# Reordering the opening of a fused attention and mixture kernel, and moving a few preparation steps of later head pairs

## The chip, the core and the metric

The kernel runs on one core of a Trainium2 chip. The metric is device microseconds (us) of one execution, the median of a few runs. The engines are named as the profile names them: PE is the matrix engine, PEld its weight loads, DVE the vector engine, ACT the scalar (activation) engine, POOL the general engine, and SP the queue from which all of this kernel's DMAs are issued. Each engine works through its own list of instructions in order; an instruction that waits holds up everything behind it in its list.

## What is computed

Three stages follow each other, all in float32:

```python
q_assign = argmax(normalize(q) @ normalize(centroids).T)      # 16 clusters, per head
k_assign = argmax(normalize(k) @ normalize(centroids).T)
mask     = q_assign[:, None] == k_assign[None, :]
scores   = where(mask, q @ k.T / sqrt(64), -1e9)               # 2 x 8 heads, 768 x 768
x        = softmax(scores) @ v                                 # tokens x 512
h        = x @ w_in;  x = (max(h, 0) + alpha * min(h, 0)) @ w_out
xn       = x / rms(x) * rms_g
out      = (silu(xn @ w_gate) * (xn @ w_val)) @ w_out2
```

## The kernel before, in words

Attention works on 8 pairs of heads (`pr` 0 to 7), the two large matrix stages follow it. The order of all instructions is written out by hand: `Attention.setup` issues the opening, then `Attention.plan` puts every further step at a slot and an order within the slot, and the slots from -12 on are issued one after the other. Pair `pr` owns slots 12·pr to 12·pr+11; a slot holds the score tiles of one block of 128 keys for the two heads of a pair. The tables `THIRD`, `FOURTH` and `FIFTH` (pairs 2, 3 and 4) give the places of preparation steps relative to the pair's own first slot: an entry (-24, 4) of pair 3 stands in slot 12, after whatever has an order below 4 there.

A pair is prepared so. `load` fetches q and k, transposed (`raw`, through L456) and natural (`nat`, L454). `prep_sq` squares them on ACT (L469), and the sums of squares give the norms (`root` in the opening, L399 to L409; `rnorm` for later pairs). `prep_hi` rounds `raw` to the matrix engine's format into `stage` (L606 on ACT, for pair 0 L608 on DVE), `prep_lo` writes the residual of the rounding beside it (L614). `sims_mm` (L516) multiplies with the centroids, `sims_copy` (L521) and `sims_turn` (L527) bring the result into token order, `prep_scale` (L543) divides by the norms, and `prep_arg` (L552 to L565) makes one-hot codes `oh` of the best cluster. DMAs copy rounded values and residuals into the operands `op1` and `op2` (`prep_dma_a` L618, `prep_dma_b` L626 to L630). The codes have to get into rows 64 to 79 of `op1`; for pairs 0 and 1 that is on PE and ACT: for pair 0 `oht_direct(h)` turns the codes of head `h` by 12 small matmuls (L589) and copies them with ACT (L598 the k side, L600 the q side).

Only then can a pair start: `max_tile` (L662) multiplies rows 0 to 79 of `op1`, and DVE takes the row maximum (L666 for the first six tiles of head pair 0, L664 later), which becomes two more operand rows (`max_split` L671 to L672, `max_rows` L690, `rows_copy` L699). `st_tile` (L712, L713) makes scores, ACT takes exp (L714), `pv_tiles` (L728, L739) multiplies with v and sums.

In the opening the PE list is: `warm(6)` (L393, matmuls on zeros), a turn of the centroid norms (L348), `sims_mm(0)`, `ss_rows(0)` (L494, sums of squares over partitions), `ss_turn` (L503), `sims_turn(0)`, `spread` of the centroids (L325), `warm(3)`, `sims_mm(1)`, `ss_rows(1)`, `ss_turn` for pair 1, `warm(4)`, `oht_direct(0)`, `oht_direct(1)`, first `max_tile`. The PSUM buffers named `ps_st` are three, given out in turn: the buffer of `ss_turn` for pair 1 is the same one into which `oht_direct(1)` puts its last three of 12 matmuls. `root` for pair 1 reads that buffer on ACT (L399 and, since it keeps a copy, L403).

Of the kernel before, what the change touches and what calls it, by code (L numbers as in the profile page):

```python
# [12 lines left out]
AF = mybir.ActivationFunctionType  # L13
ALU = mybir.AluOpType
# [4 lines left out]
BIG = float(2.0 ** 60)  # L19
# [15 lines left out]
FIFTH = {  # L35
    **PAIR,
    "lo": ((-26, 2.3), (-25, 1.05)),
    "load": ((-41, 6.1), (-41, 6.2), (-39, 6.1), (-38, 6.1)),
    "sq": ((-35, 4), (-34, 4)),
    "ss": ((-34, 5), (-33, 5)),  # L40
}
FOURTH = {
    **PAIR,
    "load": ((-38, 6.1), (-38, 6.2), (-30, 6.1), (-30, 6.2)),
    "sq": ((-32, 4), (-32, 4.1)),
    "ss": ((-30, 2.2), (-30, 2.3)),
    "norm": tuple((-27 + n // 6, 5 + (n % 6) / 10) for n in range(17)),
    "hi": ((-27, 4), (-26, 4)),
# [9 lines left out]
    "sq": ((-24, 4), (-23, 4)),  # L58
    "ss": ((-24, 5), (-23, 5)),
    "norm": tuple((-21, 5.1 + n / 100) for n in range(14)) + tuple((-18, 2.41 + n / 100) for n in range(3)),  # L60
    "hi": ((-22, 4), (-21, 4)),
    "lo": ((-18, 2.46), (-14, 6)),
    "sims": ((-20, 1.65), (-18, 1.7)),
    "scale": ((-18, 2.44),),
    "arg": ((-18, 2.45), (-16, 5), (-16, 5.1), (-15, 5), (-14, 5)),
# [160 lines left out]
class Attention:  # L226
# [52 lines left out]
    def setup(self):  # L279

        nc, C, H, D = self.nc, self.C, self.H, self.D
        v, act, g = nc.vector, nc.scalar, nc.gpsimd
        n, rows = H * C, 2 * C
        cn = self.pre([n, 2, D], "cn")
        css = self.pre([n, 1], "css")
        self.sq0 = self.pre([128, D], "sq0")
        src = self.centroids.rearrange("h c d -> (h c) d")
# [29 lines left out]
        i = self.idf.rearrange("p (e g r) -> p g e r", e=2, r=32)  # L317
        hi, lo = (i[..., r:r + 1].to_broadcast([128, 2, 2, 64]) for r in range(2))
# [3 lines left out]
        def spread(cb, w, copy):  # L322

            ps = self.bk.pr()
            nc.tensor.transpose(ps[:, :w], cn[:w].rearrange("p a d -> p (a d)"), self.idf[:w, :w])  # L325
            src = ps[:, :w].rearrange("p (j e c) -> p j e c", e=2, c=C)
            for e in range(2):
                copy(out=cb[64 * e:64 * e + 64, :, C * e:C * e + C], in_=src[64 * e:64 * e + 64, :, e, :])
# [4 lines left out]
        steps, r = self.root(css, [n, 1], "c")  # L333
        self.warm(3, self.bk.pv)
        spread(self.cb0.unsqueeze(1), rows, v.tensor_copy)
        for step in steps:
            step()
        for i in range(2):
            self.prep_sq(0, i)
        self.prep_hi(0, 0)  # L340
        self.prep_lo(0, 0)
        for i in range(2):
            v.tensor_scalar(out=cn[:, i, :], in0=cn[:, i, :], scalar1=r, scalar2=None, op0=ALU.mult)
        self.prep_hi(0, 1)
        self.warm(6, self.bk.pv)
        rc = self.bk.st()
        for i in range(0, 128, rows):
            nc.tensor.matmul(rc[i:i + rows, 0:1], lhsT=self.idf[:rows, :rows], rhs=r[:rows], start=True, stop=True)  # L348
        act.copy(out=self.rc0, in_=rc[:, 0:1])
        ps = self.bk.pr()  # L350
        self.sims_mm(0, ps)
        self.prep_sq(1, 0)
        simc = self.sims_copy(0, ps, self.rc0)
        ssc = self.ss_rows(0, v.tensor_copy)
        for h in range(2):
            self.prep_dma_a(h)
        for h in range(2):
            self.prep_dma_b(h, 1)
        self.load_v(0)
        steps, rn = self.root(self.ss_turn(ssc), [128, self.T // 2, 4, 2], "n0")  # L360
        self.sims_turn(0, self.bk.st(), simc)
        spread(self.cb, n, act.copy)
        self.prep_sq(1, 1)
        for step in steps:
            step()
        self.norm[0] = None, rn
# [4 lines left out]
        ps = self.bk.st()  # L371
        self.sims_mm(1, ps)
        ssc = self.ss_rows(1, act.copy)
        self.simc[1] = self.sims_copy(1, ps, 1.0)
        self.norm[1] = self.root(self.ss_turn(ssc), [128, self.T // 2, 4, 2], "n1", True)
        act.add_instruction(mybir.InstLoadActFuncSet(name=nc.get_next_instruction_name(), act_func_set_id=EXP_AND_LN,
                                                     ins=[], outs=[]))
        act.activation(out=spare, in_=self.eps[:, 0:1], func=AF.Exp)
        self.warm(4, self.bk.pv)
        self.prep_lo(0, 1)  # L380
        for h in range(2):
            self.oht_direct(h)
        for i in range(2):
            self.prep_hi(1, i)
        v.tensor_tensor_reduce(out=pat, in0=pat, in1=self.idf, scale=1.0, scalar=0.0, op0=ALU.mult, op1=ALU.add,
# [191 lines left out]
    def oht_direct(self, h):  # L577

        nc, X = self.nc, self.T // 2
        if h:  # L580
            hi = [self.bk.pr(), self.bk.st()]
            ps = [[self.bk.st(), self.bk.st()], hi]
        else:
            ps = [b().rearrange("p a b -> p (a b)") for b in (self.bk.mx, self.bk.pv)]
            ps = [[b, b[:, self.HS:]] for b in ps]
        for i in (1, 0):
            for g in range(2):
                for x in range(X):
                    nc.tensor.matmul(ps[i][g][0:16, x * 128:(x + 1) * 128], lhsT=self.oh[0][:, x, h, :, i, g],  # L589
                                     rhs=self.idr, start=True, stop=True)  # L590
        o1 = self.op1[h][64:80]
        for i in (1, 0):
            cuts = ((0, 128), (128, self.S)) if not i else ((0, self.S),)
            parts = [(ps[i][g][:16, :self.HS], o1[:, i, sl]) for g, sl in self.halves()] if h else \
                [(ps[i][0][:16, a:b], o1[:, i, a:b]) for a, b in cuts]
            for src, dst in parts:
                if i:
                    nc.scalar.copy(out=dst, in_=src)  # L598
                else:
                    nc.scalar.activation(out=dst, in_=src, func=AF.Identity, scale=-BIG)  # L600

# [198 lines left out]
    def plan(self):  # L800
# [3 lines left out]
        def at(s, o, fn, *a):  # L804
            ev.setdefault(s, []).append((o, len(ev.get(s, [])), fn, a))
# [4 lines left out]
        for pr in range(self.NP):  # L810
            b = SLOTS * pr
            tab = (FIRST, SECOND, THIRD, FOURTH, FIFTH, PAIR)[min(pr, 5)]
            for key, fn in (("load", self.load), ("sq", self.prep_sq), ("ss", self.prep_ss), ("hi", self.prep_hi),
                            ("lo", self.prep_lo), ("sims", self.prep_sims), ("scale", self.prep_scale),
                            ("norm", self.prep_norm), ("arg", self.prep_arg), ("oht", self.prep_oht),
                            ("load_v", self.load_v)):
                for n, to in enumerate(tab.get(key, ())):
                    if to:
                        at(b + to[0], to[1], fn, pr, n)
            h = 2 * pr  # L820
            if pr == 0:
                at(-12, -1, self.prep_dma_b, 0, 2)
                at(-12, 1, self.prep_dma_b, 1, 2)
            elif pr == 1:
                at(-5, 12, self.prep_dma_a, h)
                at(-4, 12, self.prep_dma_a, h + 1)
                at(5, 2.8, self.prep_dma_oh, h)
                at(5, 2.8, self.prep_dma_oh, h + 1)
                at(6, 2.8, self.prep_dma_b, h)
                at(6, 2.8, self.prep_dma_b, h + 1)  # L830
            else:
                for e in range(2):
                    at(b - 12, 2.5, self.prep_dma_a, h + e)
                    at(b - 12, 2.5, self.prep_dma_oh, h + e)
                    at(b - 11 + e, 2.5, self.prep_dma_b, h + e)
# [539 lines left out]
```

## Time and profile before

| | us |
|---|---|
| median of 3 runs | 819.69 (819.63 to 819.71) |
| the profiled execution | 819.63 |
| its span, first to last instruction | 817.9 |
| PE busy | 809.6 (99%) |
| DVE busy | 623.7 (76%) |
| ACT busy | 335.6 (41%) |
| POOL busy | 362.1 (44%) |

Busy times of PE contain modelled ends of pipelined matmuls, so that neighbours overlap; the distance from start to start is what one costs the list. A timeline row is start, duration, engine, line, operation, destination and source, shapes, the count of merged instructions, and in brackets the idle time before it with what ended it.

### The profile page before, as it was taken

Reading aid. Unit: us, or ns where it says so; the run is one execution under the profiler, and the core shown is the slowest. Engines: PE = TensorE matmul, PEld = TensorE weight load, DVE = VectorE, ACT = ScalarE, POOL = GpSimd, SP = SyncE. Lnnn points to the kernel's source line nnn. Section 1 sums busy time; section 2 is a strip of 40 time slices with the busy share of each in tenths; the row PEclk is TensorE's granted clock in tenths of the full one; section 3 lists DMA queues with packets and bytes.
Section 4 is the critical chain, followed back from the end, with each engine's and each line's share of the span. In section 5 each row is a group of like instructions: output and inputs, shape, how many; then the busy total and the mean of one; then the engine's idle time right before and its main releaser. Section 6 shows DMA issues by size and latency. Waiting matters only on the chain.

```text
span 817.9 us, 11705 instructions
## 1 busy us (share of the span) xinstructions
PE 809.6 (99%) x4350; PEld 625.0 (76%) x4350; DVE 623.7 (76%) x1036; ACT 335.6 (41%) x652; POOL 362.1 (44%) x335
## 2 busy tenths in 40 slices
PE   8999999999999999999999999999999999999998
PEld 5565666666666888888888888888888888888887
DVE  6989999999998489999999977877555555555523
ACT  7655776666564333433434444432212221222110
POOL 3421221221213267786766772416465546554511
PEclk9999999999999999999999999999999999999999
DMA  8786655754532022232212220102121212121012
GB/s 206 201 229 181 132 154 161 171 111 115 133 114 79 1 77 78 78 103 65 88 59 75 77 78 1 51 1 78 52 77 54 76 52 77 57 73 51 1 52 103
DMA packets 23624, 74.03 MB, mean 91 GB/s; under 512 B 3600, under 2 KB 4752, under 8 KB 23568
## 3 DMA queue, kind: packets, MB, share of 16 engines
q1 hardware_dynamic: 23568, 73.29, 31.3%
q8 instruction: 34, 0.56, 0.3%
q14 instruction: 22, 0.18, 0.1%
HBM read 49.88 MB, written 3.15 MB: 65 GB/s over the span
## 4 chain that ended last, share of the span: by engine, by line
PE 96%; DVE 2%; DMA 1%; ACT 1%; issue 0%; SPq 0%; DVEq 0%; ACTq 0%
PE ps_st L1010 35%; PE ps_mx L1010 14%; PE ps_pv L1010 14%; PE ps_pv L728 8%; PE ps_pr L1010 5%; PE ps_st L712 4%; PE ps_st L713 4%; PE ps_sm L739 3%; PE ps_ma L662 3%; PE ps_mb L662 2%; DMA nat<-in_kn_dram 1%; DVE mx L666 1%; PE ps_pv L393 1%; PE ps_pr L516 1%; PE ps_pr L690 0%; PE ps_pr L782 0%
## 5 line engine op out<-in xcount | busy, mean ns | idle before, releaser
L1077 POOL TENSOR_TENSOR gl<-v,gh 128x512 fp32r<-128x512 f32 x68 | 96.0, 1412 | 143.8 <-ACT gh L1076 142.4
L1076 ACT CAST gh<-v 128x512 fp32r<-128x512 f32 x68 | 42.3, 622 | 151.9 <-DVE v L1073 83.3
L1073 DVE TENSOR_TENSOR v<-ps_st,t 128x512 f32<-128x512 f32 x36 | 24.9, 691 | 100.3 <-PE ps_st L1010 100.2
L714 ACT ACTIVATE p<-ps_st 128x384 f32<-128x384 f32 x192 | 85.3, 491 | 28.1 <-PE ps_st L713 26.6
L992 DVE SCALAR_TENSOR_TENSOR dec_a<-raw,dec_a 128x512 uint32<-128x512 uint32 x66 | 81.6, 1236 | 2.2
L728 PE MATMUL ps_pv<-p,vnat 128*64 128x384 f32 x384 | 72.6, 499 | 0.0
L1069 DVE SCALAR_TENSOR_TENSOR v<-v,alpha,t 128x512 f32<-128x512 f32 x45 | 53.0, 1177 | 21.9 <-ACT v L1068 21.8
L712 PE MATMUL ps_st<-op 128*128 128x384 f32 x192 | 67.8, 353 | 0.3 <-ACT oht L575 0.3
L1010 PE MATMUL ps_st<-x1h,stage 128*128 128x512 f32 x272 | 67.2, 389 | 0.0
L713 PE MATMUL ps_st<-op 82*128 82x384 f32 x192 | 65.0, 339 | 0.0
L1010 PEld LDWEIGHTS ps_st<-x1h,stage 128*128 128x128 f32 x272 | 51.1, 188 | 10.6
L1123 DVE TENSOR_TENSOR x<-ps_mx,x 128x1024 f32<-128x1024 f32 x36 | 43.9, 1220 | 18.7 <-PE ps_mx L1010 18.7
L664 DVE TENSOR_REDUCE mx<-ps_ma 128x1 f32<-128x384 f32 x90 | 49.7, 552 | 10.1 <-PE ps_ma L662 9.2
L798 POOL TENSOR_TENSOR x1l<-X,x1h 128x384 fp32r<-128x384 f32 x15 | 15.9, 1062 | 91.7 <-ACT x1h L795 91.7
L1010 PE MATMUL ps_st<-x1h,wvh 128*128 128x512 f32 x144 | 56.2, 390 | 0.0
L1010 PE MATMUL ps_st<-x1h,wvl 128*128 128x512 f32 x144 | 56.0, 389 | 0.0
L1010 PE MATMUL ps_st<-x1h,wih 128*128 128x512 f32 x132 | 51.6, 391 | 0.0
L1010 PE MATMUL ps_st<-x1h,wil 128*128 128x512 f32 x132 | 51.4, 389 | 0.0
L664 DVE TENSOR_REDUCE mx<-ps_mb 128x1 f32<-128x384 f32 x90 | 49.4, 549 | 0.1
L1123 DVE TENSOR_TENSOR x<-ps_pv,x 128x1024 f32<-128x1024 f32 x35 | 42.5, 1214 | 6.8 <-PE ps_pv L1010 6.8
L990 DVE TENSOR_SCALAR dec_a<-raw 128x512 uint32<-128x512 uint32 x66 | 47.6, 722 | 0.0
L995 DVE SCALAR_TENSOR_TENSOR dec_e<-raw,dec_e 128x512 f32<-128x512 uint32 x66 | 45.7, 692 | 2.3
(304 smaller groups left out, 1998.3 us busy)
## 6 DMA issues: line engine op xcount, KB each, us to landing
raw<-in_moe_w_out_dram SPq DMA_DIRECT2D x28, 512.0 KB, 3.5
op<-stage SPq DMA_DIRECT2D x32, 384.0 KB, 5.9
raw<-in_moe_w_in_dram SPq DMA_DIRECT2D x15, 512.0 KB, 3.6
raw<-in_moe_w_val_dram SPq DMA_DIRECT2D x12, 512.0 KB, 3.4
raw<-in_moe_w_gate_dram SPq DMA_DIRECT2D x12, 512.0 KB, 3.4
op<-stage SPq DMA_DIRECT2D x16, 288.0 KB, 5.9
raw<-in_qt_dram SPq DMA_DIRECT2D x8, 384.0 KB, 4.8
raw<-in_kt_dram SPq DMA_DIRECT2D x8, 384.0 KB, 5.1
```

The costliest lines, as they stand in the source:

```text
L664: nc.vector.tensor_reduce(out=mx[:, g, k:k + 1], in_=to, op=ALU.max, axis=AX.X)
L712: nc.tensor.matmul(ps, lhsT=o1[:, 1, ks], rhs=o1[:, 0, qs], start=True, stop=False)
L713: nc.tensor.matmul(ps, lhsT=o2[:, 1, ks], rhs=o2[:, 0, qs], start=False, stop=True)
L714: nc.scalar.activation(out=self.P[s][:, e], in_=ps, func=AF.Exp, scale=self.scale)
L728: nc.tensor.matmul(ps[64 * e:64 * e + 64], lhsT=self.vnat[ph // 2][:, e, t0 + y], rhs=P[y][:, e], start=t0 + y == 0, stop=t0 + y == T - 1)
L990: lambda: v.tensor_scalar(out=a, in0=top, scalar1=3, scalar2=0x3FFFFFFF, op0=ALU.logical_shift_left, op1=ALU.bitwise_and),
L992: lambda: v.scalar_tensor_tensor(out=a, in0=top, scalar=0xC0000000, in1=a, op0=ALU.bitwise_and, op1=ALU.bitwise_or),
L995: lambda: v.scalar_tensor_tensor(out=ef, in0=bot, scalar=2.0 ** -52, in1=ef, op0=ALU.mult, op1=ALU.mult),
L1010: self.nc.tensor.matmul(ps, lhsT=a, rhs=b, start=first and i == 0, stop=last and i == len(terms) - 1)
L1069: nc.vector.scalar_tensor_tensor(out=v, in0=v, scalar=self.nalpha[:, a], in1=t, op0=ALU.mult, op1=ALU.add)
L1077: nc.gpsimd.tensor_tensor(out=lo, in0=v, in1=f(hi), op=ALU.subtract)
L1123: nc.vector.tensor_tensor(out=dst, in0=ps, in1=dst, op=ALU.add)
```

## The change

- Opening: the squares of pair 0's k are cut in two halves, one for ACT and one for DVE; `prep_hi(0, 1)` follows at once; both residuals of pair 0 come directly after it; the centroids are scaled by ACT instead of DVE; `ss_rows(0)` goes ahead of the turn of the centroid norms and of `sims_mm(0)` and is copied by ACT; `sims_copy(0)` comes after the first two steps of `root`, both squares of pair 1 after `spread`; the second half of `prep_dma_b(0)` moves from slot -12 to ahead of `load_v`.
- End of the opening: `oht_direct(0)` now comes before `root` for pair 1, and the load of the exp function set after `oht_direct(1)`; the copies of `oht_direct` are cut into halves and shared between ACT and DVE.
- Pair 2: rounding of k from slot 3 to slot 2, residual of q from slot 6 to slot 12. Pair 3: squares of q from slot 4 to slot 3. Pair 4: the two loads of `raw` from slots 9 and 10 to slot 13.

```diff
 FIFTH = {
-    "load": ((-41, 6.1), (-41, 6.2), (-39, 6.1), (-38, 6.1)),
+    "load": ((-41, 6.1), (-41, 6.2), (-35, 2.7), (-35, 2.8)),
 FOURTH = {
-    "sq": ((-32, 4), (-32, 4.1)),
+    "sq": ((-33, 4), (-32, 4)),
 THIRD = {
-    "hi": ((-22, 4), (-21, 4)),
-    "lo": ((-18, 2.46), (-14, 6)),
+    "hi": ((-22, 4), (-22, 4.1)),
+    "lo": ((-12, 2.02), (-14, 6)),
...
-        for i in range(2):
-            self.prep_sq(0, i)
-        self.prep_hi(0, 0)
-        self.prep_lo(0, 0)
+        self.prep_sq(0, 0)
+        self.prep_hi(0, 0)
+        sq, raw = self.nat[0][:, 1].rearrange("p t h d -> p (t h d)"), self.raw[0][:, 1]
+        (_, s0), (_, s1) = self.halves()
+        act.activation(out=sq[:, s0], in_=raw[:, s0], func=AF.Square)
+        v.tensor_tensor(out=sq[:, s1], in0=raw[:, s1], in1=raw[:, s1], op=ALU.mult)
+        self.prep_hi(0, 1)
         for i in range(2):
-            v.tensor_scalar(out=cn[:, i, :], in0=cn[:, i, :], scalar1=r, scalar2=None, op0=ALU.mult)
-        self.prep_hi(0, 1)
+            act.activation(out=cn[:, i, :], in_=cn[:, i, :], func=AF.Identity, scale=r)
+        for i in range(2):
+            self.prep_lo(0, i)
         self.warm(6, self.bk.pv)
+        ssc = self.ss_rows(0, act.copy)
         rc = self.bk.st()
...
         self.sims_mm(0, ps)
-        self.prep_sq(1, 0)
-        simc = self.sims_copy(0, ps, self.rc0)
-        ssc = self.ss_rows(0, v.tensor_copy)
...
+        self.prep_dma_b(0, 2)
         self.load_v(0)
         steps, rn = self.root(self.ss_turn(ssc), [128, self.T // 2, 4, 2], "n0")
-        self.sims_turn(0, self.bk.st(), simc)
+        self.sims_turn(0, self.bk.st(), self.sims_copy(0, ps, self.rc0))
         spread(self.cb, n, act.copy)
-        self.prep_sq(1, 1)
+        for i in range(2):
+            self.prep_sq(1, i)
...
         self.simc[1] = self.sims_copy(1, ps, 1.0)
-        self.norm[1] = self.root(self.ss_turn(ssc), [128, self.T // 2, 4, 2], "n1", True)
+        ss = self.ss_turn(ssc)
+        self.warm(4, self.bk.pv)
+        self.oht_direct(0)
+        self.norm[1] = self.root(ss, [128, self.T // 2, 4, 2], "n1", True)
+        self.oht_direct(1)
         act.add_instruction(mybir.InstLoadActFuncSet(name=nc.get_next_instruction_name(), act_func_set_id=EXP_AND_LN,
                                                      ins=[], outs=[]))
         act.activation(out=spare, in_=self.eps[:, 0:1], func=AF.Exp)
-        self.warm(4, self.bk.pv)
-        self.prep_lo(0, 1)
-        for h in range(2):
-            self.oht_direct(h)
...
+        cuts = (0, 128), (128, self.S)
         for i in (1, 0):
-            cuts = ((0, 128), (128, self.S)) if not i else ((0, self.S),)
-            parts = [(ps[i][g][:16, :self.HS], o1[:, i, sl]) for g, sl in self.halves()] if h else \
+            parts = [(ps[i][g][:16, :self.HS], o1[:, i, sl]) for g, sl in self.halves()] if h or i else \
                 [(ps[i][0][:16, a:b], o1[:, i, a:b]) for a, b in cuts]
-            for src, dst in parts:
+            for n, (src, dst) in enumerate(parts):
+                aside = n == (1 if i else 0) and (i or not h)
                 if i:
-                    nc.scalar.copy(out=dst, in_=src)
+                    (nc.vector.tensor_copy if aside else nc.scalar.copy)(out=dst, in_=src)
+                elif aside:
+                    nc.vector.tensor_scalar(out=dst, in0=src, scalar1=-BIG, scalar2=None, op0=ALU.mult)
                 else:
                     nc.scalar.activation(out=dst, in_=src, func=AF.Identity, scale=-BIG)
...
             if pr == 0:
-                at(-12, -1, self.prep_dma_b, 0, 2)
                 at(-12, 1, self.prep_dma_b, 1, 2)
```

## Rows read from the trace of the kernel before

**Rows 1.** The page: part 1 (busy us, shares), part 4 (chain by engine), part 6 (loads).

```profile
PE 809.6 (99%) x4350; PEld 625.0 (76%) x4350; DVE 623.7 (76%) x1036; ACT 335.6 (41%) x652; POOL 362.1 (44%) x335
PE 96%; DVE 2%; DMA 1%; ACT 1%; issue 0%; SPq 0%; DVEq 0%; ACTq 0%
...
raw<-in_qt_dram SPq DMA_DIRECT2D x8, 384.0 KB, 4.8
```

**Rows 2.** Busy time by stretch: stretch, length; PE, PEld, DVE, ACT, POOL; clock, DMA share, GB/s.

```profile
0.00:10.00 10.00, 7.87 (x44) 4.67 (x44) 5.53 (x18) 5.94 (x13) 7.21 (x45) 1.00 0.61 187
17.00:23.00 6.00, 5.35 (x27) 3.78 (x27) 5.86 (x11) 4.16 (x9) 0.00 (x0) 1.00 1.03 194
23.00:30.00 7.00, 6.70 (x44) 3.90 (x45) 6.41 (x16) 4.62 (x8) 3.73 (x8) 1.00 1.04 312
```

**Rows 3.** The chain that ended last, in order of time: start, us, what.

```profile
13.71 1.28 ACT L376
15.24 0.79 ACT op L598
16.24 0.64 PE ps_pv L662 x2
16.90 2.70 DVE mx L666 x3
```

**Rows 4.** Timeline of PE in the opening.

```profile
3.26 2.93 PE L393 MATMUL ps_pv<-zero 128*128 128x512 f32 x6
7.05 0.82 PE L494 MATMUL ps_st<-nat,hs 128*32 128x384 f32 x8
8.56 0.55 PE L503 MATMUL ps_st<-idf,ssc 128*128 128x128 f32 x3 [0.69 <-DVE ssc L496]
8.94 0.49 PE L527 MATMUL ps_st<-idf,simc 128*128 128x128 f32 x3
9.27 0.27 PE L325 MATMUL ps_pr<-idf,cn 128*128 128x128 f32 x1
12.42 0.55 PE L503 MATMUL ps_st<-idf,ssc 128*128 128x128 f32 x3 [0.58 <-ACT ssc L496]
12.72 1.17 PE L393 MATMUL ps_pv<-zero 128*128 128x512 f32 x4
14.21 0.52 PE L589 MATMUL ps_pv<-idr,oh 128*16 128x128 f32 x6 [0.31 <-DVE oh L565]
```

**Rows 5.** Timeline of ACT in the opening.

```profile
4.80 1.81 ACT L469 ACTIVATE nat<-raw 128x768 f32<-128x768 f32 x2 [1.12 <-DMA raw<-in_qt_dram]
9.14 0.28 ACT L399 ACTIVATE n_y<-ps_st,eps 128x24 f32<-128x24 f32 x1 [0.87 <-PE ps_st L503]
10.11 0.84 ACT L469 ACTIVATE nat<-raw 128x768 f32<-128x768 f32 x1
11.89 0.48 ACT L496 COPY ssc<-ps_st 128x384 f32<-128x384 f32 x1 [0.94 <-PE ps_st L494]
13.54 0.16 ACT L403 COPY n_s<-ps_st 128x24 f32<-128x24 f32 x1
18.27 1.57 ACT L606 CAST stage<-raw 128x768 fp32r<-128x768 f32 x2
```

**Rows 6.** Timeline of DVE in the opening.

```profile
10.78 0.56 DVE L543 TENSOR_TENSOR sims<-ps_st,n_a 128x384 f32<-128x384 f32 x1
13.80 0.77 DVE L565 TENSOR_TENSOR oh<-code,am 128x96 fp32r<-128x96 f32 x4
```

**Rows 7.** Timeline of ACT, PE and DVE where steps of later pairs move.

```profile
34.78 0.84 ACT L469 ACTIVATE nat<-nat 128x768 f32<-128x768 f32 x1 [0.34 <-DMA nat<-in_qn_dram]
37.78 0.44 PE L712 MATMUL ps_st<-op 128*128 128x384 f32 x1 [0.33 <-ACT oht L575]
40.97 0.95 DVE L614 TENSOR_TENSOR stage<-raw,stage 128x768 fp32r<-128x768 f32 x1
60.32 0.56 DVE L543 TENSOR_TENSOR sims<-ps_pr,n_a 128x384 f32<-128x384 f32 x1 [0.95 <-PE ps_pr L527]
```

## The prediction, made before the changed kernel was run

> **What bounds the kernel now.** I read the page first. PE is busy 99% of the span, and the chain that ended last lies on PE for 96% [rows 1]; there the reader is to see that only what moves PE's list counts, and that it can be moved where PE stands still. The table of stretches [rows 2] says where that is: between 17 and 23 us DVE is busy 5.86 of 6 us, between 23 and 30 still 6.41 of 7. The chain in order of time [rows 3] tells what starts that stretch: the load of a function set on ACT (13.71, 1.28 us), the copy of the turned codes behind it (15.24), the first max tile on PE (16.24), and then row maxima on DVE one after the other from 16.90. Until the sixth maximum and its rows are there PE has little else to do, so a first maximum that comes d earlier or later moves everything behind it by about d. That is the quantity I work out, with the timelines of PE [rows 4], ACT [rows 5] and DVE [rows 6].
>
> **The opening up to the one-hot codes.** The second square of pair 0 ends at 6.61 (4.80 + 1.81) and takes about 0.85, so it began near 5.76 [rows 5]. Cut in two, ACT's half needs some 0.48 (as the copy of 384 columns in rows 5) and DVE's 0.56 (as the product in rows 6), so both are done near 6.35. PE is free from about 6.2, when the six warm-up matmuls end [rows 4]. Today three groups follow there, the turn of the centroid norms, `sims_mm(0)` and `ss_rows(0)`, and the last ends at 7.87 (7.05 + 0.82). The sums now go first, 6.4 to 7.2, ACT copies them by 7.7, and the other two groups end near 7.9; so `ss_turn` starts at 7.9 instead of 8.56 [rows 4]. ACT's n_y follows 0.58 behind it (8.56 to 9.14, rows 4 and 5): 8.5. But `sims_copy` now stands behind the two steps of `root`, near 9.05 to 9.55, and `sims_turn` needs 0.55 when PE had to wait (as `ss_turn`): 10.15. `prep_scale` starts at 10.2 instead of 10.78, and the codes, at 13.80 to 14.57 today [rows 6], come at 13.2 to 14.0. **Gain 0.55** on DVE's side. Residuals, centroid scaling and the early operand DMA fill idle time of DVE, ACT and SP; I count them at nothing, and if DVE were late with the second residual (done near 8.7), it would still be before its next step at 8.8.
>
> **What holds PE instead.** PE's list has pair 1 between the turn and the codes. Both squares of pair 1 now stand behind `sims_copy` and `spread`. `spread` starts 0.33 behind `sims_turn` (8.94 to 9.27) and takes 0.27 [rows 4], so 9.95 to 10.2; ACT's two small copies of it take 0.4, and two 768-wide passes 1.57 (the pair at 18.27, rows 5): the second square ends near 12.3 instead of 10.95 (10.11 + 0.84, rows 5). Its sums reach ACT 0.94 later today (11.89); half of them is now done ahead, so 0.75 to 0.94, 13.05 to 13.25. The turn follows 0.53 behind (11.89 to 12.42), `warm(4)` another 0.30 (12.72), and four warm-ups hold the list for about 1.0 (three distances in 1.17 less one duration of 0.4, and one more) [rows 4]. `oht_direct(0)` then begins at **14.9 to 15.1 instead of 14.21**, though the codes are there at 14.0. I take 14.95.
>
> **The added wait.** ACT copies the codes without the set load ahead of it. Its q part of 640 columns needs the second six matmuls, 0.87 behind the first start (0.36 for six and 0.52 for the next, by the first row of six, rows 4): 15.85; it lasts about 0.6 (768 columns take 0.79, rows 3), so `root` of pair 1 begins at 16.45. Today `root` takes from 13.0 (0.58 behind its turn) to 13.70, 0.70 [rows 4, 5]; now it ends at 17.15. Its last step reads the `ps_st` buffer that the last three matmuls of `oht_direct(1)` overwrite. These three wait on PE until 17.2, and queued behind them are the first max tile, the warm-ups, everything. Three at 0.06: the first max tile starts near 17.35 instead of 16.24. **Cost 1.1** (1.3 with the later start). Without that wait it would be 16.45, **0.2 late**, since 24 matmuls at 0.06 follow 14.95 in any case. The set load moves behind `oht_direct(1)`, where ACT has no reader before the first rows of maxima, after 21 us: nothing.
>
> **The moved steps.** The first stretch after 30 us at which PE waits for ACT is 37.78, 0.33 us idle [rows 7]: ACT was held for loads at 34.78 and again 1.0 later. All operand DMAs start with the rounding of pair 0's k, which comes some 0.6 earlier, while compute is 1.1 later, so these waits go, and the rows of maxima ahead of that code turn become the next limit: **gain 0.2**, between 0 and 0.33. The rounding of k goes to slot 2 and a square to slot 3 behind it; they swap places of 0.83 each on ACT, nothing net, unless the square waits for its load (below). The residual of pair 2 leaves slot 6, where it held the row maxima of slot 7 (0.95 at 40.97, rows 7); PE's own tiles are there 0.1 later, so **gain 0.1**, at most the whole 0.9. In slot 12 it falls into DVE's idle 0.95 ahead of 60.32 [rows 7], so 0 to 0.1. The two loads go from slots 9 and 10 to 13, because the buffer is read until the residual in slot 12; their first reader is in slot 18, five slots on, and such a load lands in 4.8 [rows 1]: nothing. On SP the operand copies of the odd head and the load of v queue behind them; their readers come slots later.
>
> **Sum.** 1.1 - 0.2 - 0.1 = +0.8 on the profiled execution's 819.63 (span 817.9 and 1.7 around it; the median is 819.69, the same for this purpose): **820.5**, no change that can be told: 0.2%, some 1.6 us, is about what a measurement of this kernel can tell from none.
>
> **The rivals.** (1) The buffer does not hold PE, because the buffers come round otherwise or the wait is released by the first reader: +0.2 - 0.2 - 0.1, 819.5. For it: I infer the turn of three buffers from the source; against it: nothing shown. (2) The opening is as short as the codes allow: PE is not held by pair 1, `oht_direct` starts at 13.65, and the first max tile after 24 matmuls at 15.1, 1.1 earlier. With 0.1 from the residual: 818.4. Against it stands the wait for pair 1's squares; for it, that each of my ACT steps could be a tenth shorter, though not 1.2 together. (3) As (2), and DVE's 0.9 at 40.97 counts in full because DVE, not PE, sets the pace from 23 to 42: 819.63 - 2.0 = 817.6, faster. For it: DVE's 6.41 of 7 us between 23 and 30; against it: PE's own 37.78 wait was for ACT. [...] (5) Slower, by ACT's list: the square in slot 3 waits for a load that today lands at 34.78 and the exps of slot 4 wait behind it, up to 0.9 more on PE if its score buffers run out: 821.4.
>
> **How the numbers follow.** Forecast 0.46; (1) 0.13; (2) 0.13; (3) 0.12; (4) 0.08; (5) 0.08. Faster by over 0.2% is (3): 0.12; slower (4) and (5): 0.16; within, the rest: 0.72. The forecast's own bounds are 820.2 to 820.9 (0.1 less of gains, 0.2 more of cost, or the residual in part). The range reaches (1), (2) and (5) and their tenths: 818.2 to 821.8; it leaves out (3) and (4).
>
> **What would show it.** In the changed profile: `ss_turn` of pair 0 near 7.9, scale near 10.2, codes near 13.2; the second square of pair 1 ending near 12.3 and L589 starting near 15; a gap in L589 before its last three, ended by ACT L403; the first L662 near 17.35 and the first L666 near 18.0; at slot 5 no wait of ACT on loads. An L662 before 16 makes (2) or (3) true, warm-ups 0.46 apart after 17 us (4).

## The result, and the profile after

The changed kernel takes **824.5 us** (median of 5 executions, 824.36 to 824.85), the kernel before beside it 819.71 (819.63 to 821.0): ratio 1.0056, 95% interval 1.0042 to 1.0070. It is slower by 4.8 us; 820.5 had been forecast, 818.2 to 821.8 as the range. The profiled execution took 824.85, its span 823.1 us against 817.9. Lines of helpers have moved by a few: L593 is what was L589, L603 to L607 the copies of the turned codes, L669 the max tile, L673 its row maximum, L403 to L407 the root.

Set beside each other by the groups of `pv_tiles`, the two traces differ by +5.24 at 27.3 us and by +5.13 at the end. The whole loss lies ahead of 28 us. The table of stretches (columns as in [rows 2], after):

```profile
17.00:23.00 6.00, 4.13 (x18) 3.27 (x17) 3.75 (x8) 5.14 (x11) 0.00 (x0) 0.69 1.00 216
23.00:30.00 7.00, 6.56 (x31) 5.49 (x31) 5.50 (x14) 2.87 (x7) 0.00 (x0) 0.78 1.05 299
```

Two things differ from [rows 2]: DVE, which paced this stretch with 5.86 of 6 us, is busy for only 3.75, and PE's granted clock, 1.00 before, is 0.69 and 0.78. In steps of 2 us:

```profile
17.00:19.00 2.00, 0.36 (x6) 0.19 (x4) 1.51 (x5) 1.18 (x3) 0.00 (x0) 1.00 0.92 154
19.00:21.00 2.00, 1.77 (x8) 1.71 (x8) 0.48 (x1) 1.97 (x6) 0.00 (x0) 0.57 1.12 270
23.00:25.00 2.00, 2.00 (x6) 1.71 (x6) 1.80 (x4) 0.38 (x1) 0.00 (x0) 0.50 1.03 398
```

PE is nearly idle from 17 to 19 (0.36 of 2 us) and when it works again the granted clock reads 0.57 from 19 to 21 and 0.50 from 23 to 25. The timeline of PE, after, answers to [rows 4] and the max tile of [rows 3]:

```profile
5.92 1.60 PE L498 MATMUL ps_st<-nat,hs 128*32 128x384 f32 x8
8.40 0.55 PE L507 MATMUL ps_st<-idf,ssc 128*128 128x128 f32 x3
10.13 0.55 PE L531 MATMUL ps_st<-idf,simc 128*128 128x128 f32 x3 [1.19 <-ACT simc L525]
...
14.38 0.55 PE L507 MATMUL ps_st<-idf,ssc 128*128 128x128 f32 x3 [0.58 <-ACT ssc L500]
14.68 1.17 PE L397 MATMUL ps_pv<-zero 128*128 128x512 f32 x4
15.91 0.55 PE L593 MATMUL ps_pv<-idr,oh 128*16 128x128 f32 x6
...
19.23 0.51 PE L593 MATMUL ps_st<-idr,oh 128*16 128x128 f32 x3 [1.87 <-ACT n_s L407]
19.53 0.95 PE L669 MATMUL ps_pv<-op 80*128 80x384 f32 x2
...
26.39 0.51 PE L669 MATMUL ps_mx<-op 80*128 80x384 f32 x2
```

The turned codes start at 15.91 (14.21 before), their last three matmuls wait 1.87 us for ACT's `n_s`, and the first max tile starts at 19.53 instead of 16.24 [rows 3]. Then come the maxima at a lower pace: from the first max tile to the last of the six groups 6.86 us. ACT in the same stretch, answering to [rows 5]:

```profile
6.07 0.53 ACT L342 ACTIVATE nat<-raw 128x384 f32<-128x384 f32 x1 [0.77 <-DMA raw<-in_kt_dram]
7.56 0.48 ACT L500 COPY ssc<-ps_st 128x384 f32<-128x384 f32 x1 [0.49 <-PE ps_st L498]
11.33 1.58 ACT L473 ACTIVATE nat<-raw 128x768 f32<-128x768 f32 x2
13.85 0.48 ACT L500 COPY ssc<-ps_st 128x384 f32<-128x384 f32 x1 [0.94 <-PE ps_st L498]
16.50 0.47 ACT L603 CAST op<-ps_pv 16x384 fp32r<-16x384 f32 x1 [1.78 <-PE ps_pv L593]
17.78 0.69 ACT L607 ACTIVATE op<-ps_mx 16x640 fp32r<-16x640 f32 x1 [0.81 <-DVE op L605]
18.48 0.28 ACT L403 ACTIVATE n_y<-ps_st,eps 128x24 f32<-128x24 f32 x1
19.02 0.16 ACT L407 COPY n_s<-ps_st 128x24 f32<-128x24 f32 x1
```

And DVE, answering to [rows 6]:

```profile
10.72 0.56 DVE L547 TENSOR_TENSOR sims<-ps_st,n_a 128x384 f32<-128x384 f32 x1 [0.20 <-PE ps_st L531]
13.74 0.77 DVE L569 TENSOR_TENSOR oh<-code,am 128x96 fp32r<-128x96 f32 x4
17.00 0.55 DVE L603 CAST op<-ps_pv 16x384 fp32r<-16x384 f32 x1 [2.49 <-ACT op L603]
17.47 0.27 DVE L605 TENSOR_SCALAR op<-ps_mx 16x128 fp32r<-16x128 f32 x1
20.52 0.96 DVE L673 TENSOR_REDUCE mx<-ps_pv 128x1 f32<-128x768 f32 x1 [1.98 <-PE ps_pv L669]
```

To be seen here: the codes come at 13.74, 0.06 earlier than before. The four copies ahead of the root run one after the other although two engines share them: ACT at 16.50, DVE at 17.00 once ACT is done, DVE at 17.47, ACT again at 17.78 once DVE is done.

### The profile page after: what moved, and what is told of

Read it like the earlier page. It is cut to its first block, busy times and chain, and to the rows that moved or that the text cites. A ratio compares the mean times of both kernels' runs of the same rounds, so it can differ in the third digit from the quotient of the medians.

```text
span 823.1 us, 11707 instructions
## 1 busy us (share of the span) xinstructions
PE 813.6 (99%) x4350; PEld 627.8 (76%) x4350; DVE 625.9 (76%) x1037; ACT 335.2 (41%) x653; POOL 362.2 (44%) x335
## 4 chain that ended last, share of the span: by engine, by line
PE 98%; DVE 1%; ACT 0%; issue 0%; DVEq 0%
PE ps_st L1016 35%; PE ps_mx L1016 14%; PE ps_pv L1016 14%; PE ps_pv L735 8%; PE ps_pr L1016 5%; PE ps_st L719 4%; PE ps_st L720 4%; PE ps_sm L746 3%; PE ps_ma L669 3%; PE ps_mb L669 2%; PE ps_pv L397 1%; PE ps_pr L520 1%; PE ps_pr L697 0%; PE ps_pr L789 0%; PE ps_mb L1016 0%; PE ps_st L498 0%
```

## The experiments

Theory A after this reading: the front of the opening brings the codes no earlier but lets pair 1's squares hold PE; the end puts a wait into PE's list; and this standing still of 1.87 us lowers PE's granted clock, 1.00 up to 19 us, 0.57 from 19 to 21 and 0.50 from 23 to 25. "First max" is the start of the first max tile in the profiled execution, "behind codes" how far it lies behind the start of the turned codes there, "clock" the granted clock in that profile between 17 and 23 and between 23 and 30 us. Each kernel has one profile, and the first 8 us differ from execution to execution (last section); "behind codes" does not hang on them.

| kernel | median (executions) | ratio to before, 95% | first max | behind codes | clock |
|---|---|---|---|---|---|
| before | 819.71 (5) | | 16.24 | 2.03 | 1.00, 1.00 |
| after | 824.50 (5) | 1.0056 [1.0042, 1.0070] | 19.53 | 3.62 | 0.69, 0.78 |
| e1 root first | 820.81 (10) | 1.0011 [1.0002, 1.0021] | 18.20 | 1.93 | 1.00, 1.00 |
| e2 wait filled | 822.74 (6) | 1.0031 [1.0018, 1.0043] | 19.06 | 3.62 | 1.00, 0.91 |
| e3 ACT copies alone | 823.68 (4) | 1.0047 [1.0032, 1.0062] | 19.36 | 3.10 | 0.88, 0.86 |
| e4 slots alone | 819.89 (10) | 1.0003 [0.9993, 1.0012] | 16.18 | 2.05 | 1.00, 1.00 |
| e5 squares early | 820.50 (10) | 1.0013 [1.0004, 1.0022] | 17.20 | 1.93 | 1.00, 1.00 |
| e6 end alone | 823.48 (4) | 1.0044 [1.0030, 1.0057] | 18.28 | 3.59 | 0.56, 0.89 |
| e7 late load | 819.92 (11) | 1.0003 [0.9994, 1.0012] | 16.42 | 1.56 | 1.00, 1.00 |
| e8 e7, residual early | 819.99 (11) | 1.0010 [0.9999, 1.0021] | 15.86 | 1.45 | 1.00, 1.00 |
| e9 front alone | 822.41 (11) | 1.0023 [1.0014, 1.0031] | 18.00 | 2.29 | 1.00, 1.00 |
| e10 e8, filled | 820.48 (12) | 1.0006 [0.9995, 1.0017] | 15.50 | 1.45 | 1.00, 0.74 |
| e11 before, filled | 820.05 (11) | 0.9999 [0.9990, 1.0007] | 16.64 | 2.06 | 1.00, 1.00 |
| e12 operands first | 819.37 (11) | 0.9989 [0.9980, 0.9998] | 15.85 | 1.47 | 1.00, 1.00 |

**e1: the changed kernel with `root` of pair 1 ahead of `oht_direct(0)`, as it was before.**

```diff
+        self.norm[1] = self.root(ss, [128, self.T // 2, 4, 2], "n1", True)
         self.warm(4, self.bk.pv)
         self.oht_direct(0)
-        self.norm[1] = self.root(ss, [128, self.T // 2, 4, 2], "n1", True)
         self.oht_direct(1)
```

Theory A: L593 without a gap, no fall of the clock, the first max tile near 17.8 and the stretch behind it as fast as before, 820.7 to 821.4.

> The changed kernel with one thing undone: `root` of pair 1 goes ahead of `oht_direct(0)` on ACT again; the load of the exp set stays behind `oht_direct(1)`. [...] Rival B (the late squares of pair 1 make the loss, the wait only covers them; the clock falls because PE has had little to do since 13): the clock still falls, 822.5 or more.

Timeline of PE, e1:

```profile
16.27 0.55 PE L593 MATMUL ps_pv<-idr,oh 128*16 128x128 f32 x6
17.19 0.70 PE L593 MATMUL ps_st<-idr,oh 128*16 128x128 f32 x9
18.20 0.59 PE L669 MATMUL ps_pv<-op 80*128 80x384 f32 x2 [0.30 <-issue]
22.84 0.61 PE L669 MATMUL ps_mx<-op 80*128 80x384 f32 x2
```

The nine matmuls into `ps_st` run through, the clock stays at 1.00, and first to last max group takes 4.64 us instead of 6.86. One order of two lines is worth 3.7 us. What remains, 0.9 over before, is the front's, less what the late set load gives back. (The execution profiled here took 821.39, 0.6 more than the median.)

**e2: the changed kernel with seven warm-ups in the wait.**

```diff
             for g in range(2):
+                if h and not i and g:
+                    self.warm(7, self.bk.pv)
                 for x in range(X):
```

Theory A: the first max tile still near 19.4, but no fall of the clock, which it takes for about 1.8 of the 4.8; 822.5 to 823.0.

> The changed kernel with seven more warm-up matmuls on PE in the middle of `oht_direct(1)`, ahead of its last three transposes; nothing else. They only fill the time in which PE stands still from 17.36 to 19.22. [...] Rival C (DVE's row maxima set the pace there, the clock costs nothing): 824.3 to 824.7.

Timeline of PE, e2:

```profile
17.13 1.87 PE L397 MATMUL ps_pv<-zero 128*128 128x512 f32 x7 [0.24 <-DVE op L605]
18.84 0.34 PE L595 MATMUL ps_st<-idr,oh 128*16 128x128 f32 x3
19.06 0.62 PE L671 MATMUL ps_pv<-op 80*128 80x384 f32 x2
```

The first max tile stands 3.62 behind the turned codes, as in the changed kernel, so the wait itself stands, but the clock is 1.00 between 17 and 23 and the median 1.8 lower. That separates the two: about 1.8 of the 4.8 is the clock. In this profile, the slowest of the six executions, it fell later, to 0.50 between 29 and 31 us, which took another 0.4 (the shift against before grows from +3.09 to +3.5). From the warm-ups to that fall PE's longest idle is 0.47, ahead of 20.73 and of 25.85, and the kernel before has one as long (23.04) without a fall. What brought this fall is open.

**e3: the changed kernel with the copies of `oht_direct` by ACT alone, in the pieces of before.**

```diff
-            for n, (src, dst) in enumerate(parts):
-                aside = n == (1 if i else 0) and (i or not h)
+            for src, dst in parts:
                 if i:
-                    (nc.vector.tensor_copy if aside else nc.scalar.copy)(out=dst, in_=src)
+                    nc.scalar.copy(out=dst, in_=src)
```

> The changed kernel with the copies of `oht_direct` as before, all on ACT, nothing shared with DVE. Theory A (the shared copies run one after the other, ACT, DVE, DVE, ACT, because they read the same PSUM buffers, so sharing gains nothing and hands over twice): `root` begins about 0.5 earlier, first max tile near 19.0; 824.0 if PE's clock still falls in the shorter gap, 822.3 if it doesn't. Rival D (sharing takes load off ACT): first max tile later than 19.5, 825 or more.

Timeline of ACT, e3:

```profile
16.85 0.79 ACT L602 CAST op<-ps_pv 16x768 fp32r<-16x768 f32 x1 [1.79 <-PE ps_pv L593]
17.55 0.84 ACT L604 ACTIVATE op<-ps_mx 16x128 fp32r<-16x128 f32 x2
18.40 0.28 ACT L403 ACTIVATE n_y<-ps_st,eps 128x24 f32<-128x24 f32 x1
```

From the first copy to `n_y` it takes 1.55, where the shared copies take 1.98 (16.50 to 18.48). Sharing made this path 0.43 longer. (The first max tile starts at 19.36 and not near 19.0, as the turned codes start at 16.26 here.) PE's idle is 1.43 instead of 1.87, and the clock falls all the same, a little later and for a shorter time (1.00 from 19 to 21, 0.64 from 21 to 23, 0.51 from 23 to 25 and 1.00 again from 25); the median lies between the two forecasts, nearer to the one with the fall.

**e4: the kernel before with the four changed table entries and nothing else.**

```diff
-    "lo": ((-18, 2.46), (-14, 6)),
+    "lo": ((-12, 2.02), (-14, 6)),
...
-    "load": ((-41, 6.1), (-41, 6.2), (-39, 6.1), (-38, 6.1)),
+    "load": ((-41, 6.1), (-41, 6.2), (-35, 2.7), (-35, 2.8)),
```

> The kernel before with the four moved entries of the tables alone (rounding of pair 2's k, residual of its q, squares of pair 3's q, loads of pair 4); the opening is that of before. Theory A (all of the loss lies in the opening): 819.3 to 820.0. Rival E (a moved step stalls PE): 820.5 or more.

No difference in the median, +0.2 in the trace. The moved steps play no part in the loss.

**e5: e1 with the first square of pair 1 where it was, behind `sims_mm(0)`.**

```diff
         self.sims_mm(0, ps)
+        self.prep_sq(1, 0)
...
-        for i in range(2):
-            self.prep_sq(1, i)
+        self.prep_sq(1, 1)
```

> The kernel of the first experiment (`root` of pair 1 ahead of `oht_direct(0)`) with one more thing undone: the first square of pair 1 goes back to where ACT is idle, right behind `sims_mm(0)`, the second stays behind `spread`. Theory A (what is left of the loss, 0.9 to 1.1, is PE's list held by pair 1's squares): L593 starts some 0.75 earlier than in the first experiment and the time is 819.9 to 820.3. Rival F (what is left comes from the shared copies alone): no change against the first experiment, 820.6 to 821.0.

The turned codes start at 15.27, 1.0 earlier than in e1. Of this 0.26 is the opening ahead (the turn of pair 0's sums starts at 8.49 and 8.75); the other 0.74 lies between that turn and the codes, as expected, so the squares do hold PE's list. The medians differ by only 0.3 (820.50, 820.81), and 820.50 lies in neither forecast; the direction is as expected, the size is not settled.

**e6: the kernel before with the end alone (`oht_direct(0)` ahead of the root, set load last, copies shared).**

```diff
-        self.norm[1] = self.root(self.ss_turn(ssc), ..., "n1", True)
-        act.add_instruction(mybir.InstLoadActFuncSet(...
...
+        ss = self.ss_turn(ssc)
         self.warm(4, self.bk.pv)
-        self.prep_lo(0, 1)
-        for h in range(2):
-            self.oht_direct(h)
+        self.oht_direct(0)
+        self.norm[1] = self.root(ss, ..., "n1", True)
+        self.oht_direct(1)
+        self.prep_lo(0, 1)
+        act.add_instruction(mybir.InstLoadActFuncSet(...
```

Theory A, by which the wait and the fall of the clock are the end's own: the last three turning matmuls near 17.5 after a gap of 1.8 (1.87 in the changed kernel), a lower clock behind it, 822.7 to 823.2.

> The kernel before with the end part of the change alone: `oht_direct(0)` ahead of `root` of pair 1, load of the exp set last, copies shared; squares, sums and tables are those of before. [...] Rival G (the clock falls only because the front part left PE idle more often): gap as long, no fall, 820.9 to 821.3.

Busy time by stretch, and PE's timeline, both e6:

```profile
17.00:19.00 2.00, 1.02 (x5) 1.02 (x6) 1.14 (x3) 1.93 (x7) 0.00 (x0) 0.67 0.23 89
19.00:21.00 2.00, 2.00 (x6) 1.40 (x6) 1.73 (x2) 1.98 (x4) 0.00 (x0) 0.50 0.85 186
```

```profile
14.69 0.52 PE L590 MATMUL ps_pv<-idr,oh 128*16 128x128 f32 x6 [0.31 <-DVE oh L566]
17.98 0.51 PE L590 MATMUL ps_st<-idr,oh 128*16 128x128 f32 x3 [1.87 <-ACT n_s L404]
```

The end alone costs 3.7, 0.3 more than theory A's range, with the same wait and the same clock, though here the turned codes start as soon as they are there, as before. Rival G falls.

**e9: the front alone, with the end and the slots of before.**

```diff
-        ss = self.ss_turn(ssc)
+        self.norm[1] = self.root(self.ss_turn(ssc), ..., "n1", True)
+        act.add_instruction(mybir.InstLoadActFuncSet(...
...
         self.warm(4, self.bk.pv)
-        self.oht_direct(0)
-        self.norm[1] = self.root(ss, ..., "n1", True)
-        self.oht_direct(1)
-        act.add_instruction(mybir.InstLoadActFuncSet(...
+        for h in range(2):
+            self.oht_direct(h)
```

(against the changed kernel; the copies and the tables also go back to those of before)

Theory A, by which the front costs by itself, as pair 1's squares hold PE's list: turned codes at 15.6 to 16.3, the first max tile 1.5 to 2.0 later than before with less than 0.7 of idle ahead of it, no fall of the clock, 821.2 to 821.8.

> The kernel before with the front of the new opening alone: halves of the square, early residuals and roundings, scaling on ACT, sums of squares ahead, both squares of pair 1 behind the spread of the centroids; its end (root of pair 1, load of the function set, turned codes copied by ACT alone) and the slots are those of before. [...] Rival H (the front is the good part of the change and only its end does harm): first max tile no later than 16.24, 819.0 to 819.8.

Turned codes 15.71, first max 18.00, 0.66 idle ahead of it for ACT; shift +1.75. The five executions whose mean granted clock is 0.999 or 1.000 take 821.28 to 821.56, as theory A has it; the other six, at 0.998, take 822.41 to 822.83 and put the median outside its range. What lowers the clock in these six no run shows. Rival H falls: the front makes nothing faster by itself. Front (+2.5, or +1.7 among executions at 0.999 and 1.000 on both sides) and end (+3.7) are more than the 4.8 of both; that they share PE's idle is likely and was not tried.

**e7 and e8: can any part of it be kept?** e7 is the kernel before with the load of the exp function set behind `oht_direct`; e8 has also the second residual of pair 0 and its copy in the opening, and DVE for the first 128 columns of q's codes.

```diff
-        act.add_instruction(mybir.InstLoadActFuncSet(...
-        act.activation(out=spare, in_=self.eps[:, 0:1], func=AF.Exp)
         self.warm(4, self.bk.pv)
...
             self.oht_direct(h)
+        act.add_instruction(mybir.InstLoadActFuncSet(...
+        act.activation(out=spare, in_=self.eps[:, 0:1], func=AF.Exp)
```

> The kernel before with one move: the load of the exp set and the exp that goes with it stand behind `oht_direct(1)`. Theory A (a shift of the first max tile is a shift of the whole): ACT's first copy starts at 14.77 instead of 15.24, the first max tile 0.47 earlier, 819.2 to 819.4 where before gives 819.7. Rival H (the operand copy that lands at 20.47 and 21.09 sets the first score tiles, so nothing is gained): the same as before within 0.1.

> The kernel before with the load of the exp set behind `oht_direct(1)`, the second residual of pair 0 in DVE's idle time behind the copy of the sums, its operand copy ahead of the load of v, and the first 128 columns of the q side of `oht_direct(0)` copied by DVE. Theory A: first max tile near 15.7 instead of 16.24, as early as the 24 turning matmuls allow; 819.1 (818.9 to 819.3) where before gives 819.7. Rival H (later waits, of ACT's roundings or of the loads, give it back): 819.5 to 819.8.

Neither differs from before in its median. In the profile of e7 the first max tile does come 0.47 closer behind the turned codes (1.56, 2.03 before), but these started 0.65 later than in before (14.86). The executions of e8 fall into two groups: six at a mean clock of 0.999 or 1.000 take 819.23 to 819.99, five at 0.996 or 0.997 take 821.51 to 822.54. The middle of the six, 819.5, is 0.3 below that of before at these clocks (819.8, 22 of 27). So the earlier first maximum may be worth a little, and something else takes it back in half of the executions.

**e10 and e11: three more warm-ups in PE's idle ahead of the codes, in e8 and in the kernel before.**

```diff
+        self.warm(2, self.bk.pv)
         self.norm[1] = self.root(self.ss_turn(ssc), ...)
-        self.warm(4, self.bk.pv)
+        self.warm(5, self.bk.pv)
```

> As e8, with three more warm-up matmuls: two in PE's 0.58 us of idle ahead of the turn of pair 1's sums, one more behind it (five instead of four), in the 0.31 ahead of the codes. In e8 six executions took 819.2 to 820.0 at a mean granted clock of 0.999 to 1.000, five 821.5 to 822.5 at 0.996 or 0.997. Theory J (the low ones lose PE's clock because PE stands still in the opening, and warm-ups there keep it): at most one execution in ten at a mean clock of 0.998 or less, median 819.3 to 819.7, ratio below 1. Rival K (where the clock falls doesn't hang on these idles): again three or more in ten at 0.998 or less, median 819.6 to 821.

> The kernel before with the same three more warm-ups and nothing else. Of 48 executions of the kernel before beside the first eight experiments seven had a mean granted clock of 0.997 or 0.998 and took 820.5 to 821.6. Theory J: none or one in ten at 0.998 or less, median 819.5 to 819.8. Rival K: the share stays at one or two in ten or rises, and the three warm-ups cost what does not fit into the idle, median 819.8 to 820.2.

Six of twelve executions of e10 are at 0.998 or less, 2 of 11 of e11: rival K, these idles are not the cause. But e10's profile caught the fall. Its PE timeline and its stretches:

```profile
22.72 0.33 PE L717 MATMUL ps_st<-op 82*128 82x384 f32 x1
24.20 0.41 PE L716 MATMUL ps_st<-op 128*128 128x384 f32 x1 [1.15 <-DMA op<-stage]
```

```profile
24.00:26.00 2.00, 1.60 (x7) 1.18 (x7) 0.77 (x2) 1.02 (x2) 0.00 (x0) 1.00 1.01 392
26.00:28.00 2.00, 1.98 (x6) 1.41 (x6) 1.41 (x4) 1.69 (x4) 1.60 (x2) 0.59 1.08 267
28.00:30.00 2.00, 2.00 (x7) 0.77 (x8) 1.90 (x5) 0.84 (x2) 1.73 (x5) 0.50 1.03 212
```

And the chain that ended last there (start, us, what):

```profile
15.77 8.29 DMA op<-stage
```

PE waits for the odd head's operands, a copy that was issued on SP at 15.77 and took 8.29 us to land, while the 16 DMA engines are busy for 0.99 to 1.03 of each stretch from 17 to 26. The clock reads 1.00 up to 26 and then 0.59 and 0.50. The first scores of the odd head, which read these copies, are the fourth pair of score matmuls (L712 and L713 in before). Timeline of PE, before and e8:

```profile
23.68 0.34 PE L712 MATMUL ps_st<-op 128*128 128x384 f32 x1
```

```profile
23.54 0.41 PE L715 MATMUL ps_st<-op 128*128 128x384 f32 x1
```

In the kernel before the two copies land at 22.93 and 23.39 and these scores start at 23.68 and 24.05, some 0.7 later; the scores at 23.28 and 23.50, which the next expectation names, belong to the even head. In e8 the copies are issued earlier (15.66 against 16.71) but right behind the load of v, land later, at 23.41 and 23.74, and the scores start 0.13 behind each, at 23.54 and 23.87. It is e8 that stands just at that edge.

**e12: e8 with these copies issued ahead of the load of v.**

```diff
-        self.prep_dma_b(0, 2)
+        for h in range(2):
+            self.prep_dma_b(h, 2)
         self.load_v(0)
...
-                at(-12, 1, self.prep_dma_b, 1, 2)
```

> As e8, with the operand copies of the odd head's q and k (the ones behind the rounded halves and their residuals) issued ahead of the load of v instead of behind it. In the profile of e10 PE stood still for 1.15 us at 24.20 until such a copy, issued at 15.77, had landed at 24.07, and its clock read 0.50 from 28 to 32; in the profile of before they land at 22.93 and 23.39, and the scores that read them start at 23.28. Theory L (an opening that ends earlier runs into these transfers, and the executions of e8 and e10 at a low mean clock are the ones in which the idle is long): the copies land by 22.9, no wait of PE on a DMA before 25, at most two executions in eleven at a mean clock of 0.998 or less, median 819.2 to 819.6. Rival M (the 16 DMA engines are at their full share there, so the order of issue only moves the wait to another transfer, or the low clock has another cause): again four or more in eleven at 0.998 or less, median 819.6 to 821.2.

The copies land at 21.59 and 22.17, the odd head's first score starts at 23.23, PE waits on no transfer, none of eleven executions is at 0.998 or less (0.999 and 1.000 all), and they take 818.88 to 819.83. Theory L. Timeline of PE, e12:

```profile
15.85 0.57 PE L666 MATMUL ps_pv<-op 80*128 80x384 f32 x2
23.23 0.34 PE L716 MATMUL ps_st<-op 128*128 128x384 f32 x1
```

This version is faster than both kernels, than the one before by little: ratio 0.9989, the interval just short of 1. Among executions at 0.999 or 1.000 the medians are 819.37 and, for the kernel before beside it, 819.97 (11 of 15); 0.45 of these 0.6 us the trace shows as the shift from 27 us on. The rest of the 0.9 between the whole medians is that the kernel before has executions at a low mean clock (4 of these 15 at 0.998 or less, 17 of all 92 beside the experiments). Whether those come from the same transfer is open: no profile of before caught one, and its margin is 0.7. It can't be the only cause of low executions: in e9, with six of eleven, the copies land at 22.08 and 22.57 and are first read at 25.42 and 25.79.

## Why the prediction was wrong, by its own steps

At 27.3 us the changed kernel is 5.24 late: 1.11 as forecast for the first max tile (17.35 against 16.24), 2.18 more ahead of that tile, and 1.95 between it and 27.3, where PE's granted clock is low (0.50 between 21 and 25). The two steps that failed are "Cost 1.1", a wait that was taken too short, and the clock, which was left outside the range.

**Right: the place and the kind.** All of the loss lies ahead of 28 us, and the wait forecast for the last three matmuls of `oht_direct(1)`, ended by ACT's copy of the root, is there at the line named. Rival 1, that the buffer wouldn't hold PE, is out. The set load behind the codes cost nothing by itself: e7, which moves it alone, takes 819.92 where before takes 819.82 beside it. The first max tile was the right quantity: in all eight experiments whose clock reads 1.00 to 30 us (e1, e4, e5, e7, e8, e9, e11, e12) the profiled execution is longer or shorter than that of before by the shift of this tile, within 0.35 us.

**"Gain 0.55 on DVE's side": 0.06 in this pair of profiles, and of no use.** Here k landed just ahead of 6.07, so the two halves of the square began there and not at 5.76, the sums ended near 7.5 and not at 7.2, and the turn started at 8.40 and not at 7.9. But that is one execution. In e2, with the same front, the halves began at 5.58, the turn started at 7.92, and DVE came as forecast (10.2 and 13.2):

```profile
10.24 0.56 DVE L547 TENSOR_TENSOR sims<-ps_st,n_a 128x384 f32<-128x384 f32 x1 [0.20 <-PE ps_st L531]
13.26 0.76 DVE L569 TENSOR_TENSOR oh<-code,am 128x96 fp32r<-128x96 f32 x4
```

In e1 and e3 the halves began at 5.71 and 5.72, and the codes came only at 14.10 and 14.08, as PE's first products were slower: the six warm-ups at 3.26 took 2.93 in both and 2.38 in e2, the eight sums of squares behind them 1.69 and 1.70 against 1.46. In none of them did PE use the codes when they came: it turned them at 15.44 to 16.27.

**Wrong in size: "`oht_direct(0)` then begins at 14.9 to 15.1".** 15.91, that is +0.96 against the 14.95 taken. 0.50 of it is the turn at 8.40 instead of 7.9, which e2 did not have. The other 0.46 is in every profile with this front: from the turn to the turned codes it is 7.51 or 7.52 us (after, e1, e2, e3, e9), where 7.05 was forecast and before has 5.65. In this part the step from pair 1's second square to the copy of its sums was taken as shortened by sums done ahead, and was not (0.94, as before), and the warm-ups held PE 1.23 instead of 1.0. e9 shows what the front costs alone: 821.28 to 821.56 where the clock stays, 819.7 for before at these clocks.

**Wrong in size: the added wait, "Cost 1.1".** From the start of the turned codes to `n_y` 1.50 was forecast; it was 2.57. The estimate let the q copy start as soon as its matmuls were done, as if the k copy ran beside it. In fact k and q copies followed one another on whichever engine (1.55 with ACT alone, e3), and sharing them added 0.43 of waiting of ACT for DVE and DVE for ACT. From `n_y` to the first max tile it was 1.05 instead of 0.90. So 0.96 + 1.07 + 0.15 = 2.18, which is 19.53 less the forecast 17.35. e6 has the same length with the opening of before (3.59 from the turned codes to the first max tile), and e1, without this order, 1.93.

**Wrong in chance: the clock, rival 4, 0.08.** Rival 4 was a lower clock of PE behind the idle ahead of the first max tile, on top of the wait, and it came true. That idle had been taken as 0.9 us and was 1.87, and the granted clock read 0.57 between 19 and 21 us and 0.50 between 23 and 25. The price put on it, 2.5, was the author's estimate: the six warm-ups at 3.26 run 0.46 apart and the four at 12.72 0.25 [rows 4], so 0.2 more per 512 columns, 3.2 for 12 max products of 384 columns and seven warm-ups of 512, less the 0.65 for which PE is idle between 17 and 23 [rows 2]. It had about the right size: 2.2 longer between first and last max group (6.86 against 4.64), 1.8 in the medians with the idle filled; two warm-ups in that stretch took 1.05 (at 22.34), where before has 0.63 (at 18.37). The step that failed is the use of an idle of 0.69 [rows 4], behind which the clock read 1.00, as evidence against: it says only that this idle did nothing, and the idle forecast ahead of the max tile was itself too short, by the copies above. The granted clock was 0.69 and 0.78 (17 to 23 and 23 to 30 us) with the idle of 1.87, and 1.00 where e1 removes it; that an idle brings a lower clock the trace of before did not show. What brought the fall in e2, ahead of which no idle is longer than 0.47, no run shows.

**"Gain 0.2" and "gain 0.1".** Together 0.1: the shift of 5.24 at 27.3 us is 5.13 at the end. ACT no longer waits for loads around slot 5 in the changed kernel, as forecast, and the two score matmuls of PE around the turned codes start 0.47 apart (42.46, 42.93) instead of 0.66 (37.12, 37.78). The moved steps by themselves gave nothing that can be measured (e4), and rival 5, a loss by them, is out.

**Rivals 2 and 3, an earlier first max tile by 1.1 or more.** They had a limit that the prediction didn't see. Of the odd head's copies it says that "their readers come slots later"; in the kernel before these land 0.75 and 0.66 us ahead of their readers. With a first maximum 0.4 earlier and the copies right behind the load of v (e8) nothing of this is left, and in e10, 0.7 earlier, PE waits 1.15 for them. With the copies issued first (e12) PE does not wait.

## What to carry to other kernels

Before a step is put ahead of another on a side engine, find which buffer the step behind it releases: here a root of 0.7 us, put behind four small copies, held the matrix engine's list by a buffer taken in turn, and swapping the two lines back is worth 3.7 us. Price such a wait twice, with the idle and with the matmuls behind it at the clock granted then (0.50 between 21 and 25 us here), and take the copies of one buffer as serial, even if two engines share them (here ACT to 16.97, DVE from 17.00), until a trace shows otherwise. When an opening is made shorter, look up when the transfers behind it land, not only what the engines do: e8's gain showed in the median only when e12 issued the operands first. And compare distances inside one profile, not the starts of two profiles, where the opening itself differs from execution to execution (turned codes at 15.44 to 16.27 here, with the same list on PE).

## What was not expected of the hardware

The same eight products of PE, in before and in e7:

```profile
6.33 0.89 PE L516 MATMUL ps_pr<-raw,cb 128*32 128x384 f32 x8
```

```profile
6.33 1.51 PE L516 MATMUL ps_pr<-raw,cb 128*32 128x384 f32 x8
```

- **The clock's rise in the opening differs between executions.** In the fourteen profiles of these kernels the trace's first record of the granted clock at 1.00 starts between 4.84 (e2) and 8.05 us (e1), though the table of stretches prints 1.00 from the start, and PE's first steps go with it: the six warm-ups at 3.26 take 2.38 us in e2, 2.73 in the changed kernel, whose record starts at 5.63, and 2.93 in e1. The eight products above take 0.89 us in before, where the record starts at 6.47, and 1.51 in e7, where it starts at 7.77. With the same list on PE up to there the turned codes start at 15.44 (e2), 15.91 (after) and 16.27 (e1). So a difference of that size between two single profiles of an opening needs more executions to be told from this.
- **The fall can come after the idle, while PE works again, and it lasts.** In e10 the idle of 1.15 ends at 24.20, the clock is 1.00 to 26 and 0.50 from 28 to 32; in e3 the idle of 1.43 ends at 19.15 and the clock is 1.00 to 21, 0.64 between 21 and 23 and 1.00 again from 25. In the changed kernel the idle of 1.87 ends at 19.23 and the record at 0.50 runs from 19.28 to 26.11; in e6 the idle of 1.87 ends at 17.98 and the clock is 0.67 between 17 and 19. In e2 it fell (0.50 between 29 and 31) with no idle above 0.47 since the warm-ups.
- **Two engines that read one PSUM buffer were one after the other** in this program: ACT's half 16.50 to 16.97, DVE's from 17.00; DVE's piece of `ps_mx` to 17.75, ACT's from 17.78. Whether the chip or the program's own semaphores order them was not tried.
